# Attention and SwiGLU block on one core: bias of the first four tiles by TensorE, loads of q and k moved ahead, later projection of block 0, the last block by seven products

## Chip, cores and metric

The kernel runs on one core of a Trainium2 chip. The metric is the device time of one execution in microseconds (us). The span, from the first to the last instruction of the profile, is about 1.8 us shorter. A "ratio" is the mean time of one kernel's fast runs over that of the kernel before in the same rounds on the same chip, with its 95% interval; so it is not quite the ratio of the medians that stand beside it.

## The reference

Sliding-window attention with a linear distance bias, then a gated feed-forward block, all inputs and outputs fp32:

```python
# q, k, v: 8 batches x 8 heads x 576 positions x 64
scores = q @ k.T / 8
bias   = -slope[h] * abs(i - j)                  # slope[h] = 2 ** -(h + 1)
attn   = softmax(where(0 <= i - j < 128, scores + bias, -1e9))
x      = (attn @ v) as 4608 tokens x 512
g, val = x @ w_gate, x @ w_val                   # 512 x 1536 each
out    = (g * sigmoid(g) * val) @ w_out          # 1536 x 512
```

## The kernel before

The tokens are worked on in nine blocks of 512. Attention runs in tiles of 128 queries; four tiles make a block. For each block TensorE (PE) computes 12 columns of gate and 12 of value products, then the projection with wo. Blocks 1 to 7 are projected by a Strassen scheme of seven products with halves of the matrices instead of eight; block 0 and block 8 (the last) by plain products. Attention of later tiles is interleaved with the products at a set pace: `step` counts half columns, `target` is how many attention steps should be done by then. In the profile's lines `pg` and `pv` are the accumulators (in PSUM) of gate and value, `po` that of the projection, `ps` and `psc` those of the scores; `pt` is q or k transposed, `px` is x transposed, `wo_sb` holds wo, and `osb` is a finished piece of the output.

```python
# the mask: exp(score) is multiplied by reg = exp(-slope * distance), on VectorE
def first_masks():
    nc.vector.tensor_copy(idf, idm)
    for h in sorted(range(H), key=slot):
        nc.scalar.activation(reg[:, slot(h), :], dist, AF.Exp, scale=...)
def mul(q4):                                     # inside scores(i)
    nc.vector.tensor_mul(e[:, o, :], e[:, o, :], reg[:, o, :])
# ...
# x transposed by PE, evicted by ScalarE
    nc.scalar.copy(dst, pt)
# ...
# the last tile of the last block: two halves of 256 columns, 4 stores
def last_project(n, j):
    for half in range(2):
        for m in range(NMB):
            nc.tensor.matmul(po, hT[n][:, m, j * P:(j + 1) * P], wo_sb[:, m, c], ...)
        # half 0 evicted by ScalarE, half 1 by VectorE, then two stores, SyncE and ScalarE
# ...
# loads (one software queue, in this order; load(r) is k, q, v of tile r)
    load_w(0, 256); load_w(256, 512); load(4); load_qk(5, "q"); load_w(512, 1024)
    load_qk(5, "k"); load_qk(6); load_v(5); load_w(1024, 1536)
    load_v(6); load(7); load(8)
    loaded = 9
    for a0 in (0, 6):
        nc.gpsimd.dma_start(wo_sb[:, a0:a0 + 6, :], wo2[:, a0:a0 + 6, :])
# ...
# block 0's projection comes after columns 1, 3, 5, 7 of block 1, from row group 11 of wo down to 0
# pace in block 0
    target = base + max(0, step - ALONE) + max(0, step - 16) * (32 - b1 + ALONE) / (b1 - 16)
```

The softmax here doesn't subtract the row's maximum and nothing guards it: scores larger than these inputs give would overflow.

## Time and profile before

| | before |
|---|---|
| median time | 356.19 us (356.06 to 356.53, four runs) |
| span of the profiled run | 354.5 us, granted clock 1.0 |
| PE busy | 96% of the span |

The timeline of the kernel before at its end (start, duration, engine, line, operation; "ACTq" and "SPq" are stores issued by ScalarE and SyncE; in brackets the idle time before, and what ended it):

```profile
343.40 6.29 SPq L416 DMA_DIRECT2D out_dram<-osb  x6
...
347.76 2.78 PE L426 MATMUL po<-wo_sb,hT 128*128 128x256 f16 x24
...
349.69 1.85 ACTq L433 DMA_DIRECT2D out_dram<-osb  x2
349.79 1.71 SPq L433 DMA_DIRECT2D out_dram<-osb  x2
```

### The profile page before, as it was taken

Reading aid. Unit: us, or ns where it says so; the run is one execution under the profiler, and the core shown is the slowest. Engines: PE = TensorE matmul, PEld = TensorE weight load, DVE = VectorE, ACT = ScalarE, POOL = GpSimd, SP = SyncE. Lnnn points to the kernel's source line nnn. Section 1 sums busy time; section 2 is a strip of 40 time slices with the busy share of each in tenths; the row PEclk is TensorE's granted clock in tenths of the full one; section 3 lists DMA queues with packets and bytes.
Section 4 is the critical chain, followed back from the end, with each engine's and each line's share of the span. In section 5 each row is a group of like instructions: output and inputs, shape, how many; then the busy total and the mean of one; then the engine's idle time right before and its main releaser. Section 6 shows DMA issues by size and latency. Waiting matters only on the chain.

```text
span 354.5 us, 7261 instructions
## 1 busy us (share of the span) xinstructions
PE 341.5 (96%) x2765; PEld 197.5 (56%) x2765; DVE 273.4 (77%) x599; ACT 178.9 (50%) x355; POOL 106.9 (30%) x132
## 2 busy tenths in 40 slices
PE   7889999999999999999999999999999999999995
PEld 4684555444456655565456555664665566556643
DVE  4867976997987799678986998799878965975540
ACT  6845584555555455665556455455444323332321
POOL 8966655544848445544300100000000000000000
PEclk9999999999999999999999999999999999999999
DMA  9999999999999999999995513311022101101114
GB/s 152 170 186 187 141 176 155 99 147 137 157 142 196 146 158 163 157 167 153 165 62 105 83 39 32 88 33 58 17 75 61 44 2 59 62 0 62 41 42 96
DMA packets 157763, 37.34 MB, mean 105 GB/s; under 512 B 147232, under 2 KB 153248, under 8 KB 157728
## 3 DMA queue, kind: packets, MB, share of 16 engines
q0 software_dynamic: 116224, 18.62, 79.8%
q1 hardware_dynamic: 41056, 17.97, 27.6%
q8 instruction: 21, 0.34, 0.4%
q10 hardware_dynamic: 448, 0.30, 0.3%
q14 instruction: 14, 0.11, 0.1%
HBM read 37.91 MB, written 9.44 MB: 134 GB/s over the span
## 4 chain that ended last, share of the span: by engine, by line
PE 73%; DVE 16%; ACT 7%; issue 3%; DVEq 0%; ACTq 0%
PE pv L369 20%; PE pg L369 20%; PE po L489 14%; PE av L320 4%; DVE uu L384 4%; DVE hT L391 3%; PE ps L255 3%; PE po L410 3%; DVE ex L264 3%; PE p L489 2%; ACT ex L260 2%; PE px L346 2%; ACT tt L383 2%; ACT exc L287 2%; DVE x L323 1%
## 5 line engine op out<-in xcount | busy, mean ns | idle before, releaser
L369 PE MATMUL pg<-xT,wg_sb 128*128 128x512 f16 (+2 forms) x464 | 116.0, 365 | 0.6 <-DVE uu L384 0.3
L369 PE MATMUL pv<-xT,wv_sb 128*128 128x512 f16 (+2 forms) x464 | 114.5, 364 | 0.8 <-DVE uu L384 0.4
L383 ACT ACTIVATE tt<-pg 128x512 f16<-128x512 f32 (+2 forms) x110 | 65.5, 596 | 85.2 <-PE pg L369 81.8
L384 DVE SCALAR_TENSOR_TENSOR uu<-tt,pg 128x512 f16<-128x512 f16 (+2 forms) x109 | 73.4, 674 | 34.6 <-ACT tt L383 33.9
L391 DVE TENSOR_TENSOR hT<-uu,pv 128x512 f16<-128x512 f16 (+2 forms) x110 | 74.0, 673 | 7.1 <-PE pv L369 2.2
L369 PEld LDWEIGHTS <-wv_sb 128*128 128x128 f16 x464 | 42.8, 98 | 37.4 <-issue 3.3
L369 PEld LDWEIGHTS <-wg_sb 128*128 128x128 f16 x464 | 42.5, 98 | 36.1 <-issue 3.5
L260 ACT ACTIVATE ex<-ps 128x512 f16<-128x512 f32 x96 | 50.2, 605 | 10.1 <-PE ps L255 10.1
L169 POOL DMA_DIRECT2D va<-in_v_dram x40 | 34.1, 856 | 53.0 <-PE av L320 36.9
L175 POOL DMA_DIRECT2D qn<-in_q_dram x39 | 33.6, 864 | 24.4 <-DMA qT<-qn 14.8
L175 POOL DMA_DIRECT2D kn<-in_k_dram x39 | 33.2, 859 | 25.7 <-DMA kT<-kn 18.4
L264 DVE TENSOR_TENSOR ex<-ex,m_reg 128x1024 f16<-128x1024 f16 x48 | 32.6, 687 | 10.3 <-ACT ex L260 10.3
L489 PEld LDWEIGHTS <-hT 128*128 128x128 f16 x336 | 31.8, 98 | 15.5 <-issue 3.6
L489 PEld LDWEIGHTS <-S 128*128 128x128 f16 x252 | 23.9, 98 | 11.8 <-issue 2.9
L323 DVE TENSOR_TENSOR x<-av,rec 128x256 f16<-128x256 f32 x72 | 29.0, 420 | 0.6
L489 PE MATMUL po<-T,hT 128*128 128x256 f16 x168 | 23.1, 272 | 0.5
L489 PE MATMUL po<-T,S 128*128 128x256 f16 x168 | 23.0, 273 | 0.6 <-ACT p5s L507 0.6
L287 ACT ACTIVATE exc<-psc 128x512 f16<-128x512 f32 x40 | 21.4, 608 | 3.4 <-PE psc L283 3.4
L347 ACT COPY xT<-px 128x512 f16<-128x512 f16 x24 | 14.1, 586 | 14.9 <-PE px L346 14.8
L320 PEld LDWEIGHTS <-ex 128*128 128x128 f16 x384 | 18.4, 97 | 4.9 <-issue 0.7
L320 PE MATMUL av<-va,ex 128*128 128x65 f16 x384 | 20.4, 193 | 0.5
L410 PE MATMUL po<-wo_sb,hT 128*128 128x512 f16 x84 | 19.7, 379 | 0.0
(74 smaller groups left out, 291.0 us busy)
## 6 DMA issues: line engine op xcount, KB each, us to landing
out_dram<-osb SPq DMA_DIRECT2D x32, 256.0 KB, 2.8
va<-in_v_dram POOLq DMA_DIRECT2D x32, 128.0 KB, 7.5
qn<-in_q_dram POOLq DMA_DIRECT2D x31, 128.0 KB, 8.2
kn<-in_k_dram POOLq DMA_DIRECT2D x31, 128.0 KB, 8.1
wo_sb<-in_moe_w_out_dram POOLq DMA_DIRECT2D x2, 768.0 KB, 9.3
wg_sb<-in_moe_w_gate_dram POOLq DMA_DIRECT2D x2, 512.0 KB, 10.5
wv_sb<-in_moe_w_val_dram POOLq DMA_DIRECT2D x2, 512.0 KB, 11.8
out_dram<-osb SPq DMA_DIRECT2D x6, 128.0 KB, 2.4
```

The source lines that it names most:

```text
L169: nc.gpsimd.dma_start(va[rank][p0:p1, :, 0:D], src)
L175: nc.gpsimd.dma_start(t_[p0:p1], src)
L260: nc.scalar.activation(e[:, o:o + 2, :], banks[q4][par], AF.Exp, scale=scale)
L264: nc.vector.tensor_mul(e[:, o, :], e[:, o, :], reg[:, o, :])
L320: nc.tensor.matmul(av[:, j, :], w, val, start=(n == 0), stop=(n == len(todo) - 1))
L323: nc.vector.tensor_mul(x[:, 4 * half:4 * half + 4, :], av[:, :, 0:D], rec.broadcast_to([P, 4, D]))
L369: nc.tensor.matmul(ps[:, c0:c1], w[:, kb, ms], xT[n][:, kb, c0:c1], start=(kb == 0 and c0 == 0), stop=(kb == NKB - 1 and c1 == 512), skip_ ...
L383: nc.scalar.activation(tt, pg[:, c0:c1], AF.Tanh, scale=0.5)
L384: nc.vector.scalar_tensor_tensor(out=uu, in0=tt, scalar=one if (n, m) == PIN else 1.0, in1=pg[:, c0:c1], op0=ALU.add, op1=ALU.mult)
L391: nc.vector.tensor_mul(hT[n][:, m, c0:c1], acted[(n, m)][1][:, c0:c1], pv[:, c0:c1])
L410: nc.tensor.matmul(po, hT[n][:, m, j * P:(j + 1) * P], wo_sb[:, m, :], start=(i == 0), stop=(i == NMB - 1))
L489: nc.tensor.matmul(dst, a[:, m, cols], b[:, m, :], start=(start and m == 0), stop=(m == HM - 1), skip_group_check=True)
```

## The change

The intent: take the mask multiplications of the first four tiles off VectorE's chain by adding the bias in PSUM; bring the transfers nearer to the order in which they are wanted; project block 0 later, when wo is surely there; and use the cheaper scheme of seven products for the last block too. The core of the diff:

```diff
-    return np.where((u >= 0) & (u < WIN), u, 30000).astype(np.float32)
+    return np.where((u >= 0) & (u < WIN), u, 16000).astype(np.float32)
 # --- part 1: first four tiles
     def first_masks():
-        for h in sorted(range(H), key=slot):
-            nc.scalar.activation(reg[:, slot(h), :], dist, AF.Exp, scale=...)
+        for n, h in enumerate(by_slot):          # bias = -slope * distance / scale
+            if n % 2: nc.vector.tensor_scalar_mul(to, dist, by)
+            else:     nc.scalar.mul(to, dist, by)
+    def later_masks(n, many):                    # the exps, two at a time between 22 and 26 us
 # in products():
+                for par in range(2 if early_tile else 0):
+                    nc.tensor.matmul(two[par], idm, bias[:, o:o + 2, :], start=True, stop=False)
 # in mul():
+            if early_tile:
+                return
 # 12 filler products in weighted() and 24 filler transposes of q and k removed
+        if i < FIRST: nc.vector.tensor_copy(dst, pt)     # x transposed
+        else:         nc.scalar.copy(dst, pt)
 # --- part 2: loads
-    load_v(6); load(7)
+    load_qk(7); load_v(6); load_v(7)
     load(8)
-    loaded = 9
-    for a0 in (0, 6):
-        nc.gpsimd.dma_start(wo_sb[:, a0:a0 + 6, :], wo2[:, a0:a0 + 6, :])
+    nc.gpsimd.dma_start(wo_sb[:, 6:12, :], wo2[:, 6:12, :])
+    load_qk(9); load_qk(10, "q")
+    nc.gpsimd.dma_start(wo_sb[:, 0:6, :], wo2[:, 0:6, :])
+    load_v(9); load_qk(10, "k"); load_v(10)
+    loaded = 11
 # (the third chunk of the weights is split and goes ahead of tile 4)
 # --- part 3: place of block 0's projection, and pace
-                    if m % 2 and PRE + m // 2 < 4:   # after columns 1, 3, 5, 7
+                    if m in (3, 5, 7, 9):
-                    if m in (2, 4, 6): weight_sums(m // 2 - 1)
+                    if m in (4, 6, 8): weight_sums(m // 2 - 2)
-                target = base + max(0, step - ALONE) + max(0, step - 16) * (32 - b1 + ALONE) / (b1 - 16)
+                target = base + 1.25 * max(0, step - ALONE) + 1.5 * max(0, step - 16)
 # --- part 4: the last block by seven products, its two halves alternating
-        for j in range(3):
-            for _ in project(NBLK - 1, j, ps_a, "a", 4): yield 1.0
-        yield from last_project(NBLK - 1, 3)
+        ends = [strassen(NBLK - 1, t) for t in range(2)]
+        for t in 7 * (0, 1):
+            next(ends[t]); yield 0.75
```

## The prediction

> **What bounds the kernel now.** I read the page first: the busy times, the slices, the chain by engine, then windows by stage, the waits, and the chain in order of time for the first 60 us and the last 20.
>
> ```profile
> PE 341.5 (96%) x2765; PEld 197.5 (56%) x2765; DVE 273.4 (77%) x599; ACT 178.9 (50%) x355; POOL 106.9 (30%) x132
> DMA  9999999999999999999995513311022101101114
> PE 73%; DVE 16%; ACT 7%; issue 3%; DVEq 0%; ACTq 0%
> ```
>
> TensorE is busy 96% of the span, so the bound is TensorE's own stream. A busy PE can hide small gaps, though, so I counted stalls myself: for each pair of neighbouring matmuls, the distance of their starts less columns / 2.4 GHz + 2.5 ns (half of that for the 64-row pairs that run side by side). That gives 29 us of stall in 351: 3.0 in the first 10 us, 3.1 in 10 to 20, 6.3 in 20 to 60, 4.9 in 60 to 120, and about 12 spread over the last 230. The windows by stage agree:
>
> ```profile
> 7.00:24.00 17.00, 14.71 (x244) 12.70 (x244) 11.93 (x31) 11.98 (x24) 15.30 (x19) 1.00 2.12 171
> 24.00:57.00 33.00, 30.83 (x281) 16.54 (x279) 26.81 (x58) 21.99 (x45) 19.61 (x25) 1.00 1.72 169
> 100.00:340.00 240.00, 237.57 (x1854) 138.94 (x1853) 192.02 (x412) 115.34 (x232) 42.88 (x52) 1.00 0.81 87
> ```
>
> (Columns: stretch, length, then busy PE, PEld, DVE, ACT, POOL, clock, DMA share, GB/s.) From 100 to 340 us PE idles 1%. Everything the change can win is therefore in the first 100 us and in the tail.
>
> The start is a chain of small dependent steps. In order of time:
>
> ```profile
> 13.04 0.42 DVE qT L207
> 13.47 1.20 DVE ex L264 x2
> 14.67 0.10 DVE rec L322
> ...
> 15.77 0.33 DVE kT L207
> 16.10 1.20 DVE ex L264 x2
> ```
>
> VectorE carries the chain from 12.6 to 17.9 us, and 1.2 us of each tile is the multiplication by the mask. The DMA row is full over the first 22 slices: the transfers are a second stream, which runs in order and has no slack. Issue times of the two halves of wo, and their times to landing:
>
> ```profile
> 40.36 0.83 POOL L663 DMA_DIRECT2D wo_sb<-in_moe_w_out_dram  x1 [0.29 <-DMA qn<-in_q_dram]
> 41.83 0.83 POOL L663 DMA_DIRECT2D wo_sb<-in_moe_w_out_dram  x1 [0.64 <-DMA va<-in_v_dram]
> DMA to landing us min/median/max: 7.7/7.7/7.7
> DMA to landing us min/median/max: 10.8/10.8/10.8
> ```
>
> The first half lands at 48.1, the second at 52.6; the first projection product starts at 53.8. The tail:
>
> ```profile
> 340.15 7.77 PE po L410 x36
> 347.92 2.63 PE po L426 x24
> ```
>
> **What the Trainium skill says.** "TensorE: Matmul & The Clock Gate", Wait — 56ns, not 53.3ns?: a warm matmul takes N / 2.4 GHz plus about 2.5 ns, 215.7 ns at 512 columns. The trace agrees: four of 512 take 0.86 us, 36 take 7.77, and 24 of 256 take 2.63 (109 ns each). "PSUM — Partial Sum Buffer", The four PSUM rules: a seed other than zero must be put through the PE by an identity matmul; that is just how the bias goes in here. "DMA: Bandwidth & Descriptors", Specifications: under 512 B a transfer is below line rate. The trace agrees: 147232 of 157763 packets are under 512 B, and the full queues move 150 to 190 GB/s. "VectorE: DVE Perf Modes", The perf-mode tier table: a scalar multiply of fp32 in SBUF runs at 2x, so I estimate 0.2 to 0.3 us for each bias of 256 columns.
>
> **Part 1, the first four tiles.** Removed from VectorE: six multiplications of 0.64 us (1.28 for two) and one of 0.69, 4.5 us in all, seven of them between 11.1 and 19.0. Added to it: four copies of x transposed (0.42 each, 1.7 us) and four biases at about 4.5 us, hidden before the q cast at 6.8. On PE: 14 identity products of 512 columns, 14 x 0.216 = 3.0 us added; 24 filler transposes of 0.056 (1.3 us) and 12 filler products of 0.109 (1.3 us) removed; +0.4 in a stretch where PE waits anyway. ScalarE then is the limit: 14 exps of 0.526 us (4.21 for eight) from about 9.7 (0.2 later than now, for the bias precedes the scores) end at 17.1, and no multiplication follows. Now tile 3 is ready at 18.33 + 0.69 = 19.0. So 1.9 us are offered. Two things take most of it back. The first product of wv waits for its chunk, issued at 10.80 and landed 7.0 later, at 17.8; now that product starts at 18.60. PE's work behind it is the same less fillers, so the fourth tile's transpose comes at about 22.5 for 23.3 now: 0.8 won. And the eight exps for the later masks (2.56 for eight, now at 4.44) and four mask copies (0.54 apart, now at 7.04 to 9.3) move into 22 to 31 us, between the tanh steps that PE's PSUM buffers wait for: 4.7 us more where ScalarE has some 5 us idle in 10. By my chain arithmetic the tanh of block 0's third column stands at the time it has now (26.6) and the gain returns only partly after 31.
>
> **Part 2, loads.** Bytes up to the third weight chunk are only permuted: columns 512 to 768 of the weights land earlier, q and k of tiles 4 and 5 some 2.9 us later (two chunks of about 1.45 us), about when they are wanted (26 to 27 us). q and k of 7 land one transfer earlier. The half of wo that the projection uses first (6 to 12) keeps 48.1; then q and k of 9 and q of 10 come between (3 x about 0.93), and the other half lands at 52.6 + 2.8 = 55.4. The instruction order of the changed kernel has eight products of tile 0's projection before block 1's first gate, and the seventh and eighth need that half: the gate can start at 55.4 + 0.43 + 0.1 = 55.9 at the earliest, against 56.93 now. By then four projection products (0.86 us) fewer and 11 transposes (0.61) more have been done. Net gain at block 1: 1.03 - 0.86 + 0.61 = **0.8 us**, whatever part 1 offers beyond that.
>
> **Part 3, the pace and block 0's projection (57 to 100 us).** PE's order is the same from about 62 us up to the last blocks, so only stalls can change. They sum to 3.5 us there. Now VectorE idles 2.7 us before 58.62 and is then full (9.95 and 9.47 of 10 us in 60 to 80), because the 9 us of weight sums meet the attention. The change starts the scores of tile 9 some 4 us earlier and spreads the sums two columns later. I choose to credit under a third: **1.0 us**. It is the least certain term.
>
> **Part 4, the end.** Now 7.77 + 2.63 = 10.4 us of projection. The Strassen form takes 14 x 6 = 84 products of 0.109 us = 9.2 us. That is 1.2 us less. Against it: the second product waits for the last hT (341.5 against 341.3, 0.2 us), and 12 more VectorE sums (0.42 each) in block 8's last three columns push uu or hT by perhaps 0.2. The S2 sums are ready at about 342.4, before PE comes for them at 342.9. The last eviction and store are of the same size, so the 3.9 us after the last product stay. Net **0.8 us**.
>
> Sum: 0.8 + 1.0 + 0.8 = 2.6 us. 356.2 - 2.6 = **353.6 us**, 0.7% less.
>
> **Rivals.** (a) ScalarE becomes the bound at 22 to 33 us: the late masks delay the tanh, PSUM stays full, and part 1's gain turns negative, to be recovered later or not. For it: in-order ScalarE, four exps in a row ahead of a tanh. Against it: it idles half of 20 to 30 us and 1.75 us before 32.3. Then about 355. (b) The gain is bigger: relieved of the transfers' late landings and the attention burst, most of the 6 to 7 us of stalls from 40 to 100 vanish. For it: the loads were re-ordered by someone who saw such waits. Against it: the DMA row is full either way, and none of PE's listed waits of before is for one of these loads. Then about 351. (c) The transfers are the limit and the half of wo lands later still, or q and k of 4 and 5 make PE wait: then the middle gains nothing and 355 remains from the end alone. (d) The filler was what kept the clock up: removing it lets the clock drop. The page's title above speaks of a throttle on idle windows of about 3.4 us; here the longest stall after 6 us is 0.83 us, so I leave it at a few per cent.
>
> **Range and chances.** The three terms could each be off by about 0.8 us, mostly independently, and block 1's limit is one-sided: 351.3 to 355.6. Over 2% faster needs 7.1 us, a quarter of all stalls, of which 12 us lie where the change does nothing: 0.04. Over 2% slower needs 7.1 us of new waits: 0.01.
>
> **What would show it.** Right: the exps of the first four tiles end near 17 us and the first wv product waits for its transfer; the seventh projection product starts near 55.5 on its landing; block 1's first gate near 55.9; the last 84 products take 9.2 to 9.6 us with a gap under 0.5. Wrong: block 1's gate before 55 (the transfers ran faster than I hold), a tanh later than now by more than 1 us, or a wait of PE for VectorE's sums among the last products. VectorE's busy time should rise by about 6 us (12 sums of 0.42, seven more evictions of 0.42, four copies, four biases, less the 4.5 us of multiplications), with no effect by itself.

## More of the kernel before

The prediction shows the main lines. Two more views are needed later. First, the windows by stage of the kernel before for the stretch after block 1's first gate (stretch, length, then busy PE, weight loads, VectorE, ScalarE, GpSimd, granted clock, DMA share, GB/s):

```profile
57.00:100.00 43.00, 42.27 (x316) 20.80 (x316) 37.70 (x83) 23.56 (x44) 23.13 (x29) 1.00 1.92 138
```

## The result, and the profile after

The changed kernel took 356.12 us (median; 355.39 to 356.31, four runs) against 356.19 (356.06 to 356.53, four runs): ratio 0.9993, interval 0.9975 to 1.001. That is "same", the class given 0.95, but the time lies outside the range of 351.3 to 355.6. Measured once more on another occasion, unaltered, it took 355.23 (354.92 to 356.31, five runs; ratio 0.9984, interval 0.997 to 0.9997). By these two ratios the change is worth 0.2 to 0.6 us, though the first interval includes no gain at all. Over its nine runs the changed kernel spreads from 354.92 to 356.31, 1.4 us; the kernel before spread over 0.5 in its four, and over 0.2 to 1.0 in the rounds of the experiments but for one run at 358.20.

The page of the profile after, busy times, DMA row and chain by engine:

```profile
PE 341.3 (96%) x2767; PEld 197.4 (56%) x2767; DVE 279.5 (79%) x619; ACT 178.1 (50%) x357; POOL 108.2 (31%) x134
...
DMA  9999999999999999999945513311032101101104
...
PE 70%; DMA 11%; DVE 7%; ACT 4%; POOL 4%; issue 3%; ACTq 0%; POOLq 0%; DVEq 0%
```

PE is as busy as before, VectorE 6.1 us busier, as predicted, and the DMA row is full over the same first 22 slices. The last line is the chain of work that ended last: before it was 73% PE and 16% VectorE with no transfer in it, now transfers make 11% of it. VectorE's share has more than halved, to 7%, and transfers have come in. The windows by stage after:

```profile
7.00:24.00 17.00, 16.04 (x230) 11.24 (x230) 10.07 (x30) 9.11 (x20) 13.96 (x18) 1.00 2.19 171
24.00:57.00 33.00, 29.86 (x278) 15.79 (x276) 26.74 (x59) 25.02 (x52) 21.68 (x28) 1.00 1.77 169
57.00:100.00 43.00, 42.63 (x310) 20.41 (x309) 37.76 (x82) 23.75 (x43) 23.32 (x28) 1.00 2.09 129
```

Against before: PE is busy 16.04 for 14.71 us in the first stretch (the start is tighter), but 29.86 for 30.83 in the second (something is lost there), and the third changes by 0.36. The first two stretches hold other work than before, so busy time is only a hint that a gain is made and lost again before 57 us.

To see where, I follow PE's gate products, which are the same in all versions. "First gate" is the start of the last product before one full column (4 x 512) is counted, "gate 12" that of block 1's first column (its third product, 0.43 us after the column starts), "last gate" the same of block 8's last column. All from profiled runs, us:

| | first gate | gate 12 | gate 12 to last gate | to the last product | to the end | span |
|---|---|---|---|---|---|---|
| before | 20.98 | 57.36 | 281.34 | 11.58 | 4.19 | 354.46 |
| after | 19.91 | 57.58 | 281.11 | 10.52 | 5.34 | 354.54 |
| after, second occasion | 19.89 | 56.66 | 281.12 | 10.51 | 5.09 | 353.38 |

The first gate also moves from execution to execution: it comes at 19.6 to 20.3 in the profiles of kernels with this first part (two with early masks, below, aside), and at 20.98 and 21.10 in the two without it.

The start answers to the chain that the prediction shows of before. VectorE's timeline after, at the same place:

```profile
13.20 0.42 DVE L219 COPY kT<-pt 128x512 f16<-128x512 f16 x1 [1.68 <-PE pt L214]
13.54 0.41 DVE L219 COPY qT<-pt 128x512 f16<-128x512 f16 x1
13.87 0.17 DVE L340 RECIPROCAL rec<-av 128x4 f32<-128x4 f32 x1
```

The multiplications of 1.2 us between the copies and the reciprocals are gone, and VectorE even idles 1.68 us there.

Three things stand in the table. The start gains 1.07 us. Between first gate and gate 12 that gain is lost wholly in one run and by a third in the other. And the end's gain of 1.06 us on PE is given back by 1.15 (0.90) in the tail.

**The stretch before gate 12.** PE's timeline of the kernel after from 54.6 us:

```profile
54.60 0.59 PE L436 MATMUL po<-wo_sb,hT 128*128 128x512 f16 x2
55.29 0.28 PE L364 MATMUL px<-idm,x 128*128 128x128 f16 x2
55.41 0.39 PE L214 MATMUL pt<-idm,qn 128*128 128x128 f16 x4
56.72 0.59 PE L436 MATMUL po<-wo_sb,hT 128*128 128x512 f16 x2 [0.92 <-DMA wo_sb<-in_moe_w_out_dram]
57.15 1.02 PE L390 MATMUL pg<-xT,wg_sb 128*128 128x512 f16 x4
```

The seventh product of the projection waits 0.92 us for the second half of wo (the expectations below say 1.09, counted from one product's start to the next), and the gate follows right behind it. In the second run the same products stand without a wait:

```profile
55.40 0.39 PE L214 MATMUL pt<-idm,qn 128*128 128x128 f16 x4
55.62 0.59 PE L436 MATMUL po<-wo_sb,hT 128*128 128x512 f16 x2
56.23 1.02 PE L390 MATMUL pg<-xT,wg_sb 128*128 128x512 f16 x4
```

The transfer's own record says why: it was issued at 45.7 and landed 11.0 us later, at 56.7, in the first run; issued at 44.8 and landed 10.1 us later, at 54.9, in the second. The prediction's 55.4 lies between. The later issue comes of earlier late landings in the same stream: in both runs the first half of wo is issued 0.28 us after a v lands (at 41.01 and 40.24), k of tile 9 0.53 us after the next v (at 42.56 and 41.62), and the second half of wo 2.6 us behind that.

**The tail.** The timeline of the kernel after:

```profile
347.30 3.35 SPq L428 DMA_DIRECT2D out_dram<-osb  x5
347.31 3.63 ACTq L428 DMA_DIRECT2D out_dram<-osb  x5
...
349.51 0.42 DVE L533 TENSOR_SCALAR osb<-po 128x256 f32<-128x256 f32 x1 [0.23 <-PE po L502]
```

With the two halves alternating, every result of the last block is finished only in the last four products of each half. All ten stores, 1 MB, are issued between 347.3 and 350.2, and none has landed when the last product starts at 349.20. Their records in the two traces, issue to landing:

```
before: first of the last ten 343.40 -> 345.74 (2.3 us)   last 351.04 -> 353.23 (2.2 us)
after:  first of the last ten 347.30 -> 349.36 (2.1 us)   last 350.18 -> 353.31 (3.1 us)
```

The last store is issued 0.86 us earlier and lands 0.08 us later. Of the tail's 1.15 us, 0.94 is its longer way, and 0.21 is that it is issued later after the last product (0.98 us for 0.77).

### The profile page after: what moved, and what is told of

It reads as the page before. It is cut to its first block, busy times and chain, and to the rows that moved or that the text cites. A ratio compares the mean times of both kernels' runs of the same rounds, so it can differ in the third digit from the quotient of the medians.

```text
span 354.5 us, 7294 instructions
## 1 busy us (share of the span) xinstructions
PE 341.3 (96%) x2767; PEld 197.4 (56%) x2767; DVE 279.5 (79%) x619; ACT 178.1 (50%) x357; POOL 108.2 (31%) x134
## 4 chain that ended last, share of the span: by engine, by line
PE 70%; DMA 11%; DVE 7%; ACT 4%; POOL 4%; issue 3%; ACTq 0%; POOLq 0%; DVEq 0%
PE pv L390 21%; PE pg L390 21%; PE po L502 16%; DMA wg_sb<-in_moe_w_gate_dram 4%; PE av L338 4%; DMA wo_sb<-in_moe_w_out_dram 3%; DMA va<-in_v_dram 3%; PE p L502 3%; PE ps L271 2%; PE po L436 2%; DVE hT L412 2%; DVE uu L405 1%; ACT ex L277 1%; PE px L364 1%; POOL qn L187 1%
## 5 line engine op out<-in xcount | busy, mean ns | idle before, releaser
L502 PEld LDWEIGHTS <-hT 128*128 128x128 f16 x384 | 36.5, 98 | 15.8 <-issue 3.4
L283 DVE TENSOR_TENSOR ex<-ex,m_reg 128x1024 f16<-128x1024 f16 x42 | 28.8, 688 | 8.2 <-ACT ex L277 8.1
L502 PEld LDWEIGHTS <-S 128*128 128x128 f16 x288 | 27.4, 98 | 12.3 <-issue 2.9
L502 PE MATMUL po<-T,S 128*128 128x256 f16 x192 | 26.0, 273 | 0.6 <-ACT p5s L520 0.6
L502 PE MATMUL po<-T,hT 128*128 128x256 f16 x192 | 26.1, 272 | 0.4
L271 PE MATMUL ps<-qT,kT 64*128 64x256 f16 x192 | 17.9, 273 | 0.3 <-DVE qT L219 0.2
L368 ACT COPY xT<-px 128x512 f16<-128x512 f16 x20 | 11.7, 585 | 9.6 <-PE px L364 9.5
```

Source lines behind the costliest of these rows:

```text
L271: nc.tensor.matmul(two[par][:, j, :], kT[rows, ks, pair, :], qT[rows, p:p + 2, pair, :], start=(j == 0 and not early_tile), stop=(j == 1))
L502: nc.tensor.matmul(dst, a[:, m, cols], b[:, m, :], start=(start and m == 0), stop=(m == HM - 1), skip_group_check=True)
```

## Experiments

Where a run's name begins with "a_" it is an edit of the changed kernel, with "b_" of the kernel before with one part of the change. The kernel before of the same rounds had medians of 356.14 to 356.30. Eighteen kernels ran.

### The changed kernel again, and wo in other pieces

`after_again` is the changed kernel, unaltered (numbers above).

> The changed kernel once more, unaltered, for a second profile and five more times. In the first profile the second half of wo landed at 56.7 us and a projection product waited 1.09 us for it; in three later variants with the same loads it landed at 55.2 and nothing waited. Theory V (the landing varies from run to run, so the wait is there in some executions only): 355.4 to 356.4 with a spread of about 1 us, the profile with block 1's first gate either at 56.8 (no wait) or at 57.6. Rival (the first profile was typical): the landing is at 56.5 or later again and the median is 356.1.

`a_wo84` loads 8 of wo's 12 row groups first and 4 later, so that the seventh and eighth product need only the first load. The order of instructions on PE, ScalarE and VectorE is unaltered.

```diff
-    nc.gpsimd.dma_start(wo_sb[:, 6:12, :], wo2[:, 6:12, :])
+    nc.gpsimd.dma_start(wo_sb[:, 4:12, :], wo2[:, 4:12, :])
-    nc.gpsimd.dma_start(wo_sb[:, 0:6, :], wo2[:, 0:6, :])
+    nc.gpsimd.dma_start(wo_sb[:, 0:4, :], wo2[:, 0:4, :])
```

> The changed kernel with wo cut at row 4 instead of row 6 (rows 4 to 12 first, then q and k of tile 9 and q of 10, then rows 0 to 4); the order of instructions on TensorE, VectorE and ScalarE is unchanged, only two transfers differ. In the changed kernel the seventh projection product waits 1.09 us for the second half of wo, which lands at 56.7. Theory T (the transfer took back what the first part won): products 7 and 8 now need only the first piece (landing near 50.8), the wait goes, block 1's first gate ends about 56.5 instead of 57.58, and as TensorE's order is fixed from there the end moves by nearly as much: 355.0 to 355.4 us. Rival R (the win is given back anyway, between 57 and 97 us, to VectorE or later transfers): the gate moves as said but the end stays, 355.9 to 356.3.

Measured: 355.21 (354.85 to 355.96, five runs), ratio 0.998 (0.9967 to 0.9992). The later piece landed at 57.4, no wait stood at 55.6, and gate 12 came 36.77 us after the first gate, just as in the second run of the changed kernel (36.77) and not as in the first (37.67). So the wait adds itself fully to the stretch, and taking it away restores only what the better executions of the changed kernel have anyway.

`a_wo_late` doubles the suspect: the second half of wo goes behind v of 9 and k and v of 10. Same order on the engines.

```diff
-    nc.gpsimd.dma_start(wo_sb[:, 0:6, :], wo2[:, 0:6, :])
     load_v(9); load_qk(10, "k"); load_v(10)
+    nc.gpsimd.dma_start(wo_sb[:, 0:6, :], wo2[:, 0:6, :])
```

> The changed kernel with the second half of wo loaded after v of 9, k and v of 10, some 2.8 us later; the order of instructions on PE, ScalarE and VectorE is the same. Theory W (the seventh projection product waits for that half, and the wait shifts everything behind it one for one): it lands at 57.7 to 59.8, PE waits 2.5 to 3.5 us at 55.6, block 1's first gate comes at 59 to 60 (56.7 without a wait), and the median is 2 to 3 us above the changed kernel's 355.7, so 357.7 to 358.7. Rival (the wait only takes the place of other waits in block 1, recovered by 100 us): the gate late, but the end less than 1 us later, 355.7 to 356.7.

Measured: 359.05 (357.74 to 359.89, six runs), ratio 1.0077 (1.0058 to 1.0095). The half landed at 58.4, PE waited 2.96 us, and gate 12 was 39.71 us after the first gate: 2.94 more than without a wait, one for one, as theory W says. But the total rose by more. The windows by stage of this run, and the timeline:

```profile
57.00:60.00 3.00, 1.52 (x6) 0.64 (x6) 0.00 (x0) 0.00 (x0) 0.00 (x0) 0.92 2.37 156
60.00:63.00 3.00, 3.00 (x9) 1.09 (x8) 1.74 (x4) 0.60 (x1) 0.00 (x0) 0.51 2.53 163
```

```profile
58.48 0.59 PE L436 MATMUL po<-wo_sb,hT 128*128 128x512 f16 x2 [2.96 <-DMA wo_sb<-in_moe_w_out_dram]
58.91 1.30 PE L390 MATMUL pg<-xT,wg_sb 128*128 128x512 f16 x4
60.01 1.91 PE L390 MATMUL pv<-xT,wv_sb 128*128 128x512 f16 x4
```

The granted clock (the column before the last two) is down: the trace's clock record has one stretch of 3.41 us at 0.5, from 59.52, and four products take 1.91 us instead of 1.03. That is 1.6 us more from gate 12 to the last gate (282.75 for 281.12). This wait is paid twice.

### The end

`a_end_before` undoes part 4: `last_project` is back, the sums of block 8 are gone.

> The changed kernel with the last block projected as before (36 products of 512 and 24 of 256 columns), all else kept. Theory S (the seven-product end saves 1.1 us of TensorE, but 1 MB of results is stored in the last 3 us of products and the transfers' backlog eats all of it): same time as the changed kernel, 355.9 to 356.4, with the last product about 1.1 us later and the last store landing 2.2 us after its issue instead of 3.1. Rival E (the end is worth its 0.8 to 1.1 us and something else lost as much): 356.9 to 357.3.

Measured: 355.69 (355.09 to 356.53, five runs), ratio 0.9991 (0.9979 to 1.0004). Last gate to last product 11.58, from there to the end 4.17: 15.75 us in all, where the changed kernel has 15.86 and 15.60. Part 4 is worth nothing within these numbers.

`b_end` is the opposite: part 4 alone in the kernel before.

> The kernel before with part 4 alone (the last block by seven products). Theory (the 1.1 us that PE saves are given back by the backlog of stores): last gate to last product 10.5, last product to end 5.1 to 5.4, total 356.0 to 356.4, no change. Prediction as it stood: last product to end 4.2 and total 355.1 to 355.4.

Measured: 356.10 (355.97 to 356.44, five runs), ratio 0.9997 (0.9985 to 1.0009). Last gate to last product 10.52, to the end 5.35. The same 1.1 us is won and given back.

`a_end_nostore` leaves out the stores of one half of the last block (half of the 1 MB). Its output is wrong, which doesn't matter for the time.

```diff
-        store(n, t, top, 0, DM, end)
+        if not end or t:
+            store(n, t, top, 0, DM, end)
```

(and the same for the half's other store).

> Wrong result on purpose: the changed kernel without the four stores of the first half (t = 0) of the last block, 0.5 MB of 1.0; products and evictions are the same, in the same order. Theory S: the last stores land about 2.2 us after their issue instead of 3.1, the run is 0.8 to 1.1 us shorter: 355.1 to 355.4. Rival E2 (the tail is a fixed cost after the last eviction, whatever is in flight): 356.0 to 356.3.

Measured: 354.73 (353.94 to 355.15, five runs), ratio 0.9957 (0.9945 to 0.997). PE's products are as before (10.51), and the tail is 4.03 us where the changed kernel has 5.34 and 5.09. The last store lands 2.3 us after its issue, where the changed kernel's two profiles have 3.1 and 2.9. What the tail had grown by is, in the main, the stores' backlog.

`a_end_seq` computes the left half's last five products before the right half's, so that its stores go out earlier; to do so it gives the second accumulator a PSUM bank of its own.

```diff
+        po_y = ps_f.tile([P, 2, HC], FP32, name="poy", tag="gv") if end else po
-        X, Y = po[:, 0, :], po[:, 1, :]
+        X, Y = po[:, 0, :], po_y[:, 1, :]
-        for t in 7 * (0, 1):
+        for t in (0, 1, 0, 1) + 5 * (0,) + 5 * (1,):
```

> The changed kernel with the fourteen last groups of products in another order and with one more PSUM bank each: both first and second products as now, then the five others of the left half, then the five others of the right half; the same stores, but those of the left half start about 2.6 us earlier. Theory S: the stores no longer pile up, the last one lands 2.2 to 2.5 us after its issue, TensorE ends within 0.3 us of where it does now: 355.2 to 355.6. Rival E2: 356.0 to 356.3; if products of one half wait for each other's evictions, later still.

Measured: 355.73 (355.46 to 356.61, five runs), ratio 0.9996 (0.9982 to 1.0009). The tail did fall, to 4.72, but PE lost 0.7 us (11.21). Its timeline:

```profile
345.28 1.47 ACTq L428 DMA_DIRECT2D out_dram<-osb  x2
...
346.87 0.38 ACT L518 ACTIVATE osb<-po 128x256 f32<-128x256 f32 x1 [2.95 <-PE poy L503]
...
347.31 0.81 PE L503 MATMUL po<-T,S 128*128 128x256 f16 x6 [0.52 <-ACT osb L518]
```

ScalarE has to issue two stores, until 346.75, and its eviction stands behind them; PE then waits for the eviction's PSUM bank. (The bracket names PE, but the product that is evicted had ended at 346.14; in the next version the eviction follows its product by 0.03 us.) `a_end_seq2` moves the left half's stores to SyncE.

```diff
-        store(n, t, top, 0, DM, end)
+        store(n, t, top, 0, DM, end and t)
```

> The kernel with the last five products of each half one half after the other, now with the left half's stores all issued by SyncE. In the run before, TensorE waited 0.68 us for an eviction that stood behind a store's issue on ScalarE, and the tail after the last product was 4.7 us instead of 5.3. Theory S: the wait goes, TensorE's end is the changed kernel's (10.5 us after block 8's last gate), the tail stays at 4.7 or less: 0.5 to 0.8 us less than the changed kernel of these rounds. Rival E2: the tail grows back to 5.3 and nothing is won.

Measured: 354.94 (354.49 to 356.81, six runs), ratio 0.9974 (0.9954 to 0.9993). PE 10.53, tail 4.58: 15.11 us, 0.75 less than the changed kernel's 15.86 in its first profile and 0.49 less than the 15.60 of its second. The wide range has two reasons: the profiled run, the slowest, had a wait of 1.52 us for wo again, and 0.9 us more than usual outside its span (356.81 and 354.1).

### The late masks

In the changed kernel the exponentials that build the later masks stand between block 0's tanh steps on ScalarE. `a_masks_early2` computes them right after the biases, and copies the masks on VectorE.

```diff
+        later_masks(0, 8)                        # in first_tiles, after first_masks; make_masks too
-        nc.scalar.copy(msk[0][:, :, 0:64], reg[:, :, 128:192])
+        nc.vector.tensor_copy(msk[0][:, :, 0:64], reg[:, :, 128:192])   # and three more
```

> The changed kernel with the eight exps of the later masks on ScalarE right after the biases (5.8 to 8.4 us, where it idles before the first scores) and the four mask copies on VectorE in the first tiles, not among block 0's tanh steps. The instruction order between 22 and 60 us is re-made by the scheduler. Theory M (4.7 us of late masks on ScalarE take back part of what the first tiles won): block 0's fourth to sixth gates end 0.4 to 0.9 us earlier than the changed kernel's, counted from the first, and block 1's first gate 0.3 to 0.6 earlier: 355.2 to 355.6 us. Rival L (block 0's end is set by the attention of tile 7 and by the loads): the early gates move, block 1's first gate does not, and the time stays within 0.2 us of the changed kernel's of the same rounds.

Measured: 357.50 (356.69 to 357.75, four runs), ratio 1.0034 (1.0021 to 1.0048). Slower, and confounded: the copies (0.28, 0.72, 0.27 and 0.66 us) fall into VectorE's chain at 14.7 to 16.5 and put the first gate 0.87 us later than in the changed kernel, and the scheduler then orders 22 to 60 us anew, with a wait of 1.67 us for wo until 56.63. Columns 4 and 5 did come 0.45 and 0.7 us earlier in relation to the first gate (column 6 0.27), so the late masks seem to cost something there, though the new order may have a part in it; the version doesn't pay. `a_best` adds `a_wo84` and `a_end_seq2` to it.

> The three together: wo cut at row 4, masks early, the last half after the first with SyncE's stores. If the theories T, M and S hold and their parts add up (0.3 on average, 0.4 and 0.6): 354.4 to 354.9 us. If M falls: 354.9 to 355.3.

Measured: 356.20 (355.33 to 356.74, four runs), ratio 1.0 (0.9986 to 1.0013); gate 12 again 38.06 us after the first gate, with a wait of 1.36 us for wo. This was meant to be the best version and is not.

`a_best2` is `a_wo84` with `a_end_seq2`, masks untouched.

> The changed kernel with wo loaded as 8 and 4 of its 12 row groups and the end in sequence (left half's products and stores first), no change to the masks; order of instructions as in the run of the end in sequence with SyncE's stores. Theory (two separate costs: the wait for wo, 0 to 1.1 us from execution to execution, and the tail of stores, 0.75 us): no wait at 55 us, gate 12 at 56.2 to 56.7, last product to end 4.5 to 4.7, the PE's end 10.5 to 10.6; median 354.3 to 354.8 with a range under 1 us, 0.4 to 0.5% below the kernel before. Rival (the spread comes from elsewhere): a median of 355 and a range of 2 us as before.

Measured: 354.62 (354.43 to 355.09, five runs), ratio 0.9954 (0.9941 to 0.9967). As theory expects: no wait for wo, range 0.7 us, PE 10.53 and tail 4.60. Only gate 12 came at 57.06, later than 56.2 to 56.7, because the first gate of the profiled run came at 20.30; from one to the other it took 36.76.

### Part 1 alone

`b_first` is the kernel before with part 1 alone: bias by PE, late masks, no fillers, x evicted by VectorE. Loads, pace, projection and end are as before.

> The kernel before with part 1 alone (bias by TensorE in the first four tiles, late masks, no fillers, x transposed evicted by VectorE); loads, pace and end as before. Theory (part 1 wins 1.0 us at the first gate, and the late masks and block 0's ScalarE chain take most back): first gate at 19.7 to 20.2, block 1's first gate 56.9 to 57.5 (before: 57.36), total 355.7 to 356.3. Rival (the early gain is kept until something in part 2 takes it): block 1's first gate at 56.3, total 355.1.

Measured: 354.75 (354.62 to 354.90, five runs), ratio 0.9958 (0.9946 to 0.9969). **My theory fell.** I had expected the late masks to take the early gain back. Instead first gate 19.77, gate 12 at 55.95 and span 353.00: of 1.21 us won at the first gate nothing is lost, and 0.2 more is won behind it. PE's timeline of this run ahead of gate 12 has no wait for wo and one small one for VectorE:

```profile
52.52 1.89 PE L431 MATMUL po<-wo_sb,hT 128*128 128x512 f16 x8 [0.24 <-DVE exc L314]
...
55.33 0.22 PE L214 MATMUL pt<-idm,kn 128*128 128x128 f16 x1
55.52 1.02 PE L390 MATMUL pg<-xT,wg_sb 128*128 128x512 f16 x4
```

So one part alone brings 1.5 us, and the whole change 0.2 to 0.6. With part 4 worth nothing, parts 2 and 3 together must cost 0.9 to 1.3 us. `a_end_before`, which is parts 1 to 3, says the same without assuming that parts add up: ratio 0.9991 against 0.9958 here, 1.2 us, though in other rounds.

### Loads, pace and the projection's place, each undone

`a_loads_before` is the changed kernel with the old order of loads. The order of PE, ScalarE and VectorE is unaltered.

> The changed kernel with the load order of the kernel before (wo whole after tile 8, q and k of 9 and 10 when their turn comes); PE, ScalarE and VectorE have the same order as in the changed kernel. Theory W (the moved half of wo is what spreads the times; the rest of the loss comes of the order on the engines): halves of wo land at 48 to 49 and 52 to 53.5, no wait at 55.6, first gate to block 1's first gate 36.7 to 36.8 as in the changed kernel's runs without a wait, times within 0.6 us of each other, median 355.0 to 355.3. Rival L (the new order of loads also holds up block 0): that stretch falls to 36.2 and the median to 354.5 or less. Rival E (tiles 9 and 10 are needed early): PE waits for q or k of 9 or 10 after 57 us and the median is over 355.5.

Measured: 359.51 (358.17 to 360.36, six runs), ratio 1.0091 (1.0074 to 1.0107). wo was there in time (48.2 and 52.5), yet it is the slowest run of all:

```profile
51.09 0.28 PE L364 MATMUL px<-idm,x 128*128 128x128 f16 x2 [0.66 <-DVE x L341]
...
58.01 0.61 PE L214 MATMUL pt<-idm,qn 128*128 128x128 f16 x4 [2.32 <-DMA qn<-in_q_dram]
```

PE waits 2.32 us for a tile of q that landed at 57.96, and runs at a granted clock of 0.66 and 0.77 in the two windows from 57 to 63. Rival E is right, only earlier than it said: the changed order on PE transposes two tiles of q before block 1's first gate, and without the new loads they are not there. The new loads are needed; they pay for q with wo.

`a_pace_before` undoes the pace alone (the one line of `target`).

> The changed kernel with the pace of the attention as before (one step of attention for each half column up to the 16th, then two), loads and later projection as changed. Theory P (the new pace puts the last exponentials and multiplications of block 0 in the way, and that is the 0.6 us by which the stretch from first gate to block 1's first gate is longer than with part 1 alone): that stretch falls to 36.0 to 36.3 where no wait for wo falls in it, median 354.8 to 355.2. Rival (the projection moved behind is what leaves PE without work there): the stretch stays at 36.7 or more, median 355.2 to 356.

Measured: 358.00 (356.01 to 358.61, six runs), ratio 1.0039 (1.0019 to 1.0059):

```profile
55.73 0.59 PE L436 MATMUL po<-wo_sb,hT 128*128 128x512 f16 x2 [2.20 <-DMA wo_sb<-in_moe_w_out_dram]
```

The two waits for VectorE's x, which the changed kernel shows and its edits show near there, are gone. The first of them in the changed kernel (the second, of 0.32 us, is at 51.90):

```profile
50.97 0.29 PE L364 MATMUL px<-idm,x 128*128 128x128 f16 x2 [0.66 <-DVE x L341]
```

Theory P holds in mechanism. Gate 12 is 38.53 us after the first gate, which less the wait of 2.20 is 36.33, 0.03 above its 36.0 to 36.3. This order has three more projection products (0.65 us) ahead of the gate than the changed kernel (11 for 8), so like for like it is 35.68 against the 36.77 of the changed kernel without a wait: the old pace saves 1.1 us there. But the products now reach the seventh of the projection sooner, and wait there until wo lands at 55.7. The time saved became a new wait. The median overstates the loss: three of the six runs have 0.8 to 1.5 us more than usual outside the span, and the spans have a median of 355.1, where the changed kernel's nine have 354.0 and the kernel before 354.4. The profile is of the fastest of the six.

`a_proj_before` undoes the projection's place alone (and that of the weight sums).

> The changed kernel with block 0's projection and the weight sums where the kernel before has them, loads and pace as changed. Rival R (the later projection takes the filler work away from block 0's end): PE has 11 products before block 1's first gate again, and with wo there in time it would take 36.2 us from gate to gate; but its seventh and later products come for the second half of wo before it has landed, so I expect a wait of 1 to 3 us and a median of 356 to 358. Theory P (the pace alone is at fault): the same wait, as the products stand at most as early; the stretch longer than 37.5.

Measured: 356.65 (354.82 to 358.56, six runs), ratio 1.0011 (0.9984 to 1.0037), the widest range of all. PE waits for wo, which landed at 56.8:

```profile
56.81 0.81 PE L436 MATMUL po<-wo_sb,hT 128*128 128x512 f16 x3 [1.94 <-DMA wo_sb<-in_moe_w_out_dram]
```

Gate 12 is 38.80 us after the first gate; less the wait that is 36.86, not rival R's 36.2, and the two waits for x are still there (0.66 and 0.32). So the pace seems to cost here too.

`best5` has part 1, the mended end, the old pace and the old loads (wo's halves swapped), and the new, later projection.

> The run before it with the later projection of the changed kernel, pace and order of loads as before the change but for the swapped halves of wo. Theory T (it is the later projection that puts the transposes of q of 9 and 10 ahead of block 1's first gate, and so needs them loaded ahead): PE waits 1.5 to 3 us for q at 55 to 58, block 1's first gate 38 to 39.5 after the first gate, median 355.8 to 357.5. Rival (with the old pace they are there in time): no wait, 36.0 to 36.4, median 353.8 to 354.4.

Measured: 358.50 (356.18 to 358.72, six runs), ratio 1.0048 (1.0024 to 1.0073). Theory T holds in mechanism, with a wait just over its 1.5 to 3 us, gate 12 later than it said (40.78 us after the first gate) and a time above its range:

```profile
58.46 0.61 PE L214 MATMUL pt<-idm,qn 128*128 128x128 f16 x4 [3.15 <-DMA qn<-in_q_dram]
```

It is the later projection that lets the transposes of q go ahead of block 1's first gate. The order of instructions says the same: between first gate and gate 12 every profile with the later projection has 28 transposes of q, every one with the earlier projection 20; the eight are two tiles more. `a_proj_before` and `best5` change this by the projection's place alone. With it, q of two more tiles must be loaded before that gate, and with q loaded first, wo is late. The kernel before doesn't meet the question.

### What adds up

`best3` is part 1 with the mended end of `a_end_seq2`; loads, pace and projection as before.

> The kernel before with part 1 and with the end in sequence (left half of the last block's seven products first, its stores on SyncE's queue): the two parts that the runs so far show to pay, without the new load order, pace and later projection. Theory (the two gains are separate stretches and add): block 1's first gate 55.7 to 56.2, last gate to last product 10.5, last product to end 4.5 to 4.6, median 353.8 to 354.2. Rival (the end's gain is within the noise or needs the other parts): 354.6 to 354.9 as part 1 alone.

Measured: 354.38 (354.21 to 354.95, five runs), ratio 0.995 (0.9938 to 0.9962). Between theory and rival: gate 12 is at 56.22, the tail is 4.83 and not 4.5 to 4.6, and the profile shows a wait of 0.64 us, because the projection starts with wo's upper half, which the kernel before loads second. `best4` swaps the two loads.

```diff
-    for a0 in (0, 6):
+    for a0 in (6, 0):
```

> The run of part 1 with the end in sequence, its two halves of wo loaded in the other order (the half that the projection uses first now lands first, at 48 instead of 52.7); order on the engines the same. Theory W (the first projection product stood 0.2 to 0.6 us for that half): no wait for wo at 52.5, block 1's first gate 0 to 0.4 us earlier in relation to the first gate (36.2 or less), median 353.9 to 354.3. Rival (VectorE's last multiplication of block 0 ends at the same time and takes the wait's place): the same 354.2 to 354.5.

Measured: **353.96 us** (353.83 to 355.09, six runs; the 355.09 has the span of the others, 352.1), ratio 0.9931 (0.9913 to 0.9949). First gate 19.62, gate 12 at 55.52, PE's end 10.53, tail 4.84, span 352.13. The windows show PE without a gap just where the changed kernel stood (1.99 of 3.00 there):

```profile
54.00:57.00 3.00, 3.00 (x18) 1.40 (x16) 0.29 (x2) 1.78 (x3) 2.32 (x4) 1.00 2.45 153
```

This version beats the kernel before by 0.7%, and its median is below both of the changed kernel's (356.12 and 355.23, in other rounds). It keeps part 1, part 4 in another order, and one swapped pair of loads.

## Why the prediction was wrong

The class was right, but any change of less than 7 us would have had it. Much of the mechanism was right too; the sum was too large. For block 1's gate, the stretch behind it and the end it promised 0.8 + 1.0 + 0.8 us. In the same terms, with the 0.25 us of work that the later projection moves from the first stretch to the second, the first profile gives -0.5, 0.5 and -0.1 (in all -0.08), the second 0.45, 0.5 and 0.15 (1.08). So block 1's gate and the tail failed, and the middle was too large by half. Step by step:

- **Part 1: right in size, wrong in what becomes of it.** Offered were 1.9 us, 0.8 won at the fourth tile; the first tanh came at 21.76 for 22.83, 1.07 earlier. Two details failed: the exponentials ended at 18.2 and not at 17.1, because they began at 9.90 and not 9.7 and ScalarE stood another 0.38 and 0.60 us for later scores; and the chunk of wv landed at 16.83, so the first product of wv, at 17.76, did not wait for it. (The four biases on VectorE, estimated at 0.2 to 0.3 us each, took 0.27, 0.28, 0.59 and 0.76 for the same shape. They were not quite hidden: the first k cast comes at 6.00 for 5.25, the q cast at 6.87 for 6.79.) "The gain returns only partly after 31" is refuted: alone, part 1 has 1.41 us at gate 12 and keeps it. It could be kept; parts 2 and 3 prevent that. This is the step that I did not see at all: I took part 2's landing as a ceiling over part 1's gain, which it is, but asked nowhere whether the changed order needs to wait for that landing.
- **Part 2, gate of block 1: the landing was a number where it should have been a spread, and a second wait was missed.** "The gate can start at 55.9 at the earliest" is the right mechanism: the seventh product waits, and the gate follows. The gate started at 57.15 with the wait and at 56.23 without it. The landing moved between 54.9 and 56.7 in two runs of the same kernel, and even with wo in time the gate is 0.3 us late, for PE stood 0.66 and 0.32 us for VectorE's x. The new pace comes to its last gate column of block 0 early (column 11 at 46.93, with the old pace at 48.0 to 48.1 where part 1 is in), and with the old pace the two waits are gone. The kernel before has 0.23 and 0.32 there.
- **Part 3: mis-sized by half.** From gate 12 to the last gate 0.23 us were won. The 0.25 us of work that the later projection owes lies in this stretch too, so stalls fell by 0.5, not by 1.0. "I choose to credit under a third" had no wait behind it that a view names.
- **Part 4: PE right, tail wrong.** PE's part fell by 1.06 us, near the 1.2 less 0.2 to 0.4 of the prediction. The step that failed is "the last eviction and store are of the same size, so the 3.9 us after the last product stay". The size is the same, but what is in flight ahead of it is not: when the last product started, four of the last ten stores had landed before, none after. From the last product's start (4.19 us before; 3.9 from its end) the tail grew by 1.15 us (0.90).
- **Rivals.** (c), the transfers as the limit, comes nearest: of fourteen profiles with the later projection eight show PE waiting for wo or q ahead of gate 12, and in the other six, `after_again` among them, wo landed less than a microsecond before it was wanted or a smaller piece was asked for. (a), the late masks, was not what lost the gain; `b_first` has them and loses nothing. (b) did not come. (d) did not come: the clock stays at 1.0 without the fillers, as the prediction expected. The experiments show how near it was: in the three with waits of 2.3 us and more it fell to half for 3.41 us.
- **A reading.** The prediction says that the full queues move 150 to 190 GB/s; its page's first twenty slices show 99 to 196.

What stays open: why the same transfer lands 1.8 us apart in two executions (issue 0.9 us later, and 0.9 us longer under way). The trace leads the first half back to two loads of v that landed 0.8 and 0.9 us later; why they did, no run touched. In the nine profiles with this order of loads the half of wo lands between 54.9 and 57.0, and the changed kernel wants it at 55.6. The spans go with it: those of kernels that come close to the landing spread over 1.0 to 2.8 us, those of `a_wo84` and `a_best2`, where the wait is taken away, over 0.8 and 0.6, and those with loads and projection as before (`b_first`, `b_end`, `best3`, `best4`) over 0.3 to 0.6; the kernel before stays within 1.0 but for one run, of 356.3.

## What to carry to other kernels

A stream of transfers that is full has no early place for everything: moving one load ahead makes another late, so ask for each moved load what now waits for it, and test each part alone before adding them. Where a wait's end varies from run to run, predict it as a range, and keep the consumer clear of that range (here 2 us wide). At the end of a kernel it is not the last store that counts but how many are in flight with it; finish results one after the other rather than all at once.

## What the Trainium skill lacked or had wrong

- "TensorE: Matmul & The Clock Gate", What's actually happening, gives one idle window of about 3.4 us as what lowers the clock, and Why this matters for your kernels advises no gaps over about 3 us. Here the clock fell to 0.5 for 3.41 us with single waits of 2.32, 2.96 and 3.15 us, but not with waits of 1.94 and 2.20. PE was not idle all through the window: in the 3.41 us before the fall it was busy for 31%, 31% and 20%, and in the profiles without a fall no such stretch after the first 8 us was under 36%. The limit itself was not measured, but 3 us is not safe here.
- "DMA: Bandwidth & Descriptors", Anatomy of one DMA, gives a fixed cost of about 2.0 us for one transfer issued by GpSimd. The stores here were issued by SyncE and ScalarE; the last took 2.2 us in the kernel before, but 3.1 us with all ten stores (1 MB) issued within 2.9 us. No page that I read sizes this backlog for the end of a kernel; here the tail grew by 0.9 to 1.2 us.
- No page that I read says how far the landing of one transfer moves from execution to execution in a full queue: 10.1 and 11.0 us under way, 54.9 and 56.7 us on the clock, for the same kernel.
